# Batch 0's P V from the transposed p in place, on 32-row tiles, in an attention and gated-MLP kernel on one Trainium2 core

## The chip, the core and the metric

The kernel runs on one core of a Trainium2 chip. The core has five engines that run side by side, each with its own queue of instructions, executed in order: TensorE (PE in the profile; its weight loads are listed apart as PEld), VectorE (DVE), ScalarE (ACT), GpSimd (POOL) and SyncE (SP), which here only issues DMAs. Data lie in SBUF, on 128 partitions; matmuls write to PSUM, of which this kernel uses eight banks of 128 x 512 fp32. Engines wait for each other through semaphores. The metric is the device time of one execution in microseconds; the median of several runs is given, and one further execution is profiled.

## The reference

```python
scores = scale * np.matmul(q, k.transpose(0, 1, 3, 2))          # 8 batches, 8 heads, 576 x 64
mask_local = (rel >= 0) & (rel < 32)
mask_strided = (rel >= 0) & (pos[None, :] % 32 == pos[:, None] % 32)
masks = [mask_local if h < 4 else mask_strided for h in range(8)]
attn = softmax(where(masks, scores, -1e9))
x = (attn @ v).transpose(0, 2, 1, 3).reshape(8, 576, 512)
h = np.maximum(x @ w_in, 0.0)                                    # 512 -> 1024
u, v = h[..., :512], h[..., 512:]
v_n = (v - mean(v)) / sqrt(var(v) + 1e-6)
v_s = einsum('ts,bsd->btd', w_spatial, v_n) + b_spatial          # 576 x 576
return (u * v_s) @ w_out                                         # 512 -> 512
```

Four heads attend to a window of 32 positions back, four to the positions that are equal modulo 32. Then comes an MLP whose second half is normalised, mixed over positions and multiplied with the first.

## The kernel before

The kernel works through 8 batches. Attention is done for two heads at a time: pair `t` is batch `t // 4`, and of the four pairs of a batch the first two are local and the last two strided. So batch 0 is t = 0, 1 (local) and t = 2, 3 (strided).

A **local pair** (`local_attention`, L445) cuts the 576 queries into 18 blocks of 32. Each block needs 64 keys: its own 32 and the 32 before. The scores of the blocks are put side by side and on top of each other: five slots of columns, and within a slot up to four blocks in the four quarters of 32 partitions (`local_blocks` says which block lies where). After the softmax, p is a tile of 128 x (10 x 64). VectorE's transpose works on squares of 32 x 32 (L541) and writes the result to `pc`: each quarter then holds, transposed, the p of the blocks that lie in it. Before, this was not multiplied where it lay. Twelve copies (L548 to L562, helper `rnd`, lines L368 on ACT and L370 on DVE or POOL) moved quarters to other partitions and built `ptl`, in which 96 queries share one stationary 128 rows of v: three blocks and their four key blocks, with zeros where they don't meet. Then 12 matmuls of 128 rows, 64 columns of v and 96 queries (L570) wrote x, transposed, to two banks of PSUM, half of the queries each.

A **strided pair** (`strided_attention`, L585) has 32 residues with 18 positions each. After the transpose (L657), four copies (L661) built `pts`, block-diagonal in the same way, and 16 matmuls of 128 rows and 72 queries (L673) wrote two banks.

**Two rounded parts.** x is needed as a sum of two rounded parts, so `evac_x` (L401) makes of each bank a rounded copy (L390 or L392) and a subtraction on DVE (L378) that gives the remainder. The same splitting into two parts is done to the weights as they arrive (`weight`, L724: L746 on ACT, L754 on POOL, L762 on DVE, then `rnd` and L378): w_in arrives in eight blocks (u and v, four each), w_out in four, w_spatial in four and a tail. Each product of the MLP is then three matmuls. Every fp32 matmul of the program that isn't of this rounded type shows as two in the trace.

The **MLP** of a batch: L878 makes the v half, 128 positions a time (the last 64 positions in a tail); L920 the u half; L1001, with L1013 and L1014 for the tail, the mixing over positions, for which all of v must have been normalised and w_spatial split; L1043 multiplies with w_out. Batches overlap: attention of later batches is put between the products of earlier ones.

**What sets the order.** Nothing is ordered by hand. `Program.order` (L169) simulates the five engines with fixed costs. Each operation has a key, and an engine that is free in the simulation takes the ready operation with the lowest key. The instructions are then issued in that order; on the chip each engine's queue runs in it. The table `KEYS` (L40) gives the keys: `"a"` for the first eight pairs, `"u"`, `"v"`, `"o"` for the blocks of w_in and w_out, `"s"` and `"t"` for w_spatial, `"cst"` for the mask constants, `"fill"` for the clearing of tiles; a DMA of a pair or a weight has a key some 20 to 34 below it. `"lead"` shifts the keys of later pairs against the MLP's. Where the simulation sees PE idle for long in the first 110 us, filler matmuls on zeros are issued (L1178). The tables `tiled` and `FETCHED` hold small matmuls back where too many would follow one another.

**Buffers.** `r_po` (L357) has two banks for P V; a new user waits until both readers of the old one are done. `r_pc` has one place for the transposed p, `r_v` two for v, `r_q` two for q. `w_out_sb` (L325) is a tile of its own. t = 2 has its v in a borrowed place (`v_third`).

Of the kernel before, what the change touches and what calls it, by code (L numbers as in the profile page):

```python
# [10 lines left out]
F32R = mybir.dt.float32r  # L11
# [7 lines left out]
B, H, S, D = 8, 8, 576, 64  # L19
DM = H * D  # L20
DFF = 1024
HF = DFF // 2
P = 128
STRIDE = 32
# [5 lines left out]
LS = 5  # L30
# [8 lines left out]
NT = 4  # L39
KEYS = {  # L40
    "a": (-1153.0, -1248.4, -1132.6, -528.4, 173.8, 237.2, 196.5, 305.5,),
    "v": (-479.4, -798.9, -798.5, -237.5,),
    "u": (165.3, -36.7, -381.8, -468.5,),
    "s": (2276.1, 559.3, 2950.2, 2726.0,),
    "t": (1026.5,),
    "o": (800.1, 780.6, 949.7, 806.1,),
    "cst": (-1235.7,),
    "lead": (-1.2,),
    "fill": (261.3, 1164.3, -1850.5, -198.5, 42.5, 203.7,),
    "dp": (742, -13288,),  # L50
    "dpt": (254.9,),
    "near": (331.04,),
# [3 lines left out]
OTHER_BANK = (1, 2, 3)  # L56
FETCHED, FETCH_COST = 200.0, 32.0
# [252 lines left out]
def attention_moe(ctx, tc, qT, kT, vl, vs, cst, eye, w_in, w_out, wsp, wtail, out):  # L310
# [14 lines left out]
    w_out_sb = sb.tile([P, 2, NT, DM], F32R, name="w_out_sb")  # L325
# [27 lines left out]
    at_raw, at_minus = r_o.new(), r_o.new()  # L353
    minus = lambda: at_minus()[:, :P].bitcast(F32R)
# [41 lines left out]
    def load(key, dst, src, writes, nbytes, reads=()):  # L396
        add(key, [(DMA, nbytes / DMA_RATE)], lambda eng: eng.dma_start(dst(), src), reads, writes)
# [30 lines left out]
    def mask_scores(due, s_ps, parts):  # L428


        def f(eng):
            at = 0
            for i, k, n in parts:
                eng.matmul(
                    s_ps()[:, at : at + n * k].rearrange("p (n k) -> p n k", k=k), minus(),
                    masks(i, k)[:, None, :].to_broadcast([P, n, k]), start=at == 0, stop=False,
                )
                at += n * k

        add(  # L440
            due - 14.5, [(PE, 80 + pe_cost(P, sum(k * n for _, k, n in parts)))], f,
            [(at_minus,), (at_minus, "masks")], [(s_ps,)], spare=(s_ps, s_ps),
        )

    def local_attention(t, due, q, kl, v, vin, kin):  # L445
# [82 lines left out]
        if t in APART:  # L528
# [8 lines left out]
        pc = r_pc.new()  # L537
# [6 lines left out]
            pin, [(pc,)],  # L544
        )
        ptok = []
        ptl_c = ptl.rearrange("p (c j) q -> p c j q", j=2)
        for i, n, slot, c0, z in LOCAL_MOVES:  # L548
            for k in range(2):
                src = slice(STRIDE * z, STRIDE * (z + 1))  # L550
                dst = slice(STRIDE * (i + k), STRIDE * (i + k + 1))
                rnd(
                    due - 5, 2 * n * STRIDE,
                    lambda i=i, n=n, c0=c0, dst=dst: ptl_c[
                        dst, c0 : c0 + n, :, STRIDE * i : STRIDE * (i + 1)
                    ],
                    lambda k=k, n=n, slot=slot, src=src: turned()[
                        src, slot : slot + n, :, STRIDE * k : STRIDE * (k + 1)
                    ],
                    [(pc,), ("ptl0",)], [("ptl", i, k, c0)], blocks=True,  # L560
                )
                ptok.append(("ptl", i, k, c0))  # L562
# [22 lines left out]
    def strided_attention(t, due, q, k, v, vin, kin):  # L585
# [30 lines left out]
        if not masked:  # L616
# [36 lines left out]
        pc = r_pc.new()  # L653
# [3 lines left out]
            lambda eng: eng.transpose(turned(), pp[:]), [ptok], [(pc,)],  # L657
        )
        for i in range(4):
            r = slice(STRIDE * i, STRIDE * i + STRIDE)  # L660
            rnd(  # L661
                due - 5, nu * RA, lambda r=r, i=i: pts[r, :, i],
                lambda r=r: turned()[r, :, :RA], [(pc,), ("pts0",)], [("pts", i)], blocks=True,
            )
# [30 lines left out]
    def attention(t, due):  # L695
# [3 lines left out]
        if t == 2:  # L699
            place = v_third  # L700
            v = lambda: f32(place()).rearrange("p a b c -> p (a b c)").rearrange("p (u d) -> p u d", d=D)
        else:
            v = place = r_v.new()
        load(due - 34, q, qT[b, hp], [(q,)], P * SP * 4)
        if local:
            k = r_k.new()
            load(due - 33, k, kT[b, hp], [(k,)], P * (STRIDE + S) * 4)
            load(due - 20, lambda: v()[:, : 2 * LB, :], vl[b, hp], [(place,)], P * 768 * 4)
            kin = [(k,)]
        else:  # L710
# [5 lines left out]
            load(due - 20, v, vs[b, hp - 2], [(place,)], P * 1024 * 4)  # L716
            kin = [("k", t % 2, j) for j in range(2)]
        xs[t] = r_x.new()
        (local_attention if local else strided_attention)(t, due, q, k, v, [(place,)], kin)

    def x_tok(t):
        return [(xs[t], i, c0) for i in range(2) for c0 in ((0, 3) if t % NHP < 2 else (0, 1))]
# [49 lines left out]
    def weights():  # L772
        jobs = []
        for i in range(NT):
            rows = slice(i * P, (i + 1) * P)
            for c, name in enumerate("uv"):
# [6 lines left out]
                KEYS["o"][i], w_out[rows, :], DM, lambda j, i=i: w_out_sb[:, j, i], ("w_out", i),  # L783
# [4 lines left out]
        for job in jobs:  # L788

            def put(job=job):  # L790
                what = "w_out" if job[4][0] == "w_out" else "w_in"
# [9 lines left out]
            yield job[0], put  # L801
# [181 lines left out]
    def moe_2(b, key):  # L983
# [50 lines left out]
        def project(hf, k0):  # L1034
            c0 = b * S + hf * HS
            g = gs.pop(hf)
            for e in range(NT):
                o_ps = r_pm.new()
                for f in range(NT):

                    def fn(eng, e=e, f=f, o_ps=o_ps):
                        for i, (w, a) in enumerate(PROD):
                            eng.matmul(  # L1043
                                o_ps()[:, :HS],
                                w_out_sb[:, w, f, e * P : (e + 1) * P],
# [7 lines left out]
                        [(g[0], f), (g[1], f), ("w_out", f, 0), ("w_out", f, 1)], [(o_ps,)],  # L1053
# [133 lines left out]
def _layout(q, k, v, w_in, w_spatial, b_spatial, w_out):  # L1187
# [21 lines left out]

    cst = np.zeros((P, 3, 2 * STRIDE), np.float32)  # L1210
# [7 lines left out]
    def words(w):  # L1218
# [12 lines left out]
        "vl": vl,  # L1231
        "vs": vs,
# [26 lines left out]
```

## Time and profile before

| | |
|---|---|
| median of 3 runs | 529.55 us (527.65 to 531.61) |
| the profiled execution | 528.65 us |
| its span, first to last instruction | 526.9 us |
| mean granted TensorE clock | 0.997 |
| ACT, POOL busy | 244.5, 85.7 us |
| share of the chain that ended last | L1043 20%, L1001 19%, L920 17%, L878 17% |

The chain of work that ended last is PE's for 88% of the span. The profile gives each engine's busy time in any stretch of the span, its instructions in order of time (with the idle time ahead of one and what ended it, in brackets), and groups of instructions by line and shape. In the timeline a row is: start, length, engine, line, operation, output<-inputs, shape, count. A row that merges several instructions has the time from the first start to the last end. "issue" in brackets means that the engine waited for nothing that the profile shows.

### The profile page before, as it was taken

To read this page: it belongs to the slowest core of one execution; us is meant where nothing else is said; L and a number is where in the kernel's file an instruction comes from. 1 tells how busy PE (TensorE), PEld (TensorE's weight loads), DVE (VectorE), ACT (ScalarE), POOL (GpSimd) and SP (SyncE) were. 2 spreads that over 40 slices of the span, in tenths; PEclk is the share of its full clock that TensorE was granted. 3 is DMA by queue.
4 is the path that set the end of the run, shared out by engine and by line. 5 is a ranking of instruction groups with operands and counts; after the bars stand their busy time and mean duration, and the time that the engine had idled before them with its cause. 6 is when DMAs were issued, how large, how long until landed. Compare 5 with 4: busy or idle time off the path is not lost.

```text
span 526.9 us, 14624 instructions
## 1 busy us (share of the span) xinstructions
PE 514.0 (98%) x6002; PEld 471.0 (89%) x6002; DVE 317.1 (60%) x1004; ACT 244.5 (46%) x753; POOL 85.7 (16%) x170
## 2 busy tenths in 40 slices
PE   8899899899999999999999999999999999999997
PEld 4569699789899898998999899998999899998997
DVE  3999997594862867716256677954268252426132
ACT  6769665556553664724433473522234242213111
POOL 1643421121120213201010032111002020001000
PEclk9999899999999999999999999999999999999999
DMA  7978633622252223410223324310022200110011
GB/s 260 323 271 259 220 110 101 207 92 90 70 171 81 89 84 121 164 46 0 79 79 123 111 79 163 117 46 24 0 73 70 85 1 1 46 46 1 1 46 45
DMA packets 26242, 52.65 MB, mean 100 GB/s; under 512 B 3136, under 2 KB 11584, under 8 KB 26176
## 3 DMA queue, kind: packets, MB, share of 16 engines
q1 hardware_dynamic: 26176, 51.72, 29.6%
q8 instruction: 47, 0.77, 0.6%
q14 instruction: 19, 0.16, 0.1%
HBM read 42.27 MB, written 9.44 MB: 98 GB/s over the span
## 4 chain that ended last, share of the span: by engine, by line
PE 88%; DVE 7%; ACT 2%; issue 1%; DMA 1%; POOL 1%; DVEq 0%; ACTq 0%; POOLq 0%
PE m L1043 20%; PE m L1001 19%; PE m L920 17%; PE m L878 17%; PE po L673 3%; PE po L570 3%; PE s L460 2%; PE m L1013 2%; PE s L603 2%; PE m L1014 2%; PE m L1178 1%; DVE w_in_sb L378 1%; DMA q<-qT 1%; DVE vn L378 1%; ACT pl L517 1%
## 5 line engine op out<-in xcount | busy, mean ns | idle before, releaser
L1001 PE MATMUL m<-wsp_sb,vn 128*128 128x288 f32 x768 | 112.7, 298 | 2.0 <-DVE wsp_sb L378 1.5
L1001 PEld LDWEIGHTS m<-wsp_sb,vn 128*128 128x128 f32 x768 | 106.5, 191 | 3.2 <-DVE wsp_sb L378 2.0
L1043 PE MATMUL m<-g,w_out_sb 128*128 128x288 f32 x768 | 106.6, 297 | 0.0
L920 PE MATMUL m<-x,w_in_sb 128*128 128x288 f32 x768 | 106.2, 297 | 0.0
L920 PEld LDWEIGHTS m<-x,w_in_sb 128*128 128x128 f32 x768 | 103.3, 188 | 1.6
L1043 PEld LDWEIGHTS m<-g,w_out_sb 128*128 128x128 f32 x768 | 103.5, 188 | 0.6
L878 PE MATMUL m<-w_in_sb,x 128*128 128x512 f32 (+1 forms) x408 | 100.0, 398 | 2.1 <-issue 1.4
L878 PEld LDWEIGHTS m<-w_in_sb,x 128*128 128x128 f32 (+1 forms) x408 | 74.2, 185 | 22.9 <-issue 2.4
L390 ACT COPY o<-m 128x288 f32<-128x288 f32 x60 | 23.8, 399 | 90.3 <-PE m L1043 73.0
L854 POOL TENSOR_TENSOR bn<-bn,sel 128x1 f32<-128x1 f32 (+1 forms) x37 | 20.7, 560 | 188.4 <-DVE bn L849 185.0
L378 DVE TENSOR_TENSOR x<-po,x 128x288 fp32r<-128x288 f32 x64 | 27.5, 447 | 38.5 <-ACT x L390 38.1
L1023 DVE TENSOR_TENSOR u<-m,u 128x288 f32<-128x288 f32 x64 | 28.1, 452 | 37.2 <-PE m L1014 36.8
L370 POOL TENSOR_SCALAR ptl<-pc 32x320 f32<-32x320 f32 (+3 forms) x71 | 29.0, 408 | 128.4 <-PE po L570 69.2
L517 ACT ACTIVATE pl<-pl,ml 128x64 f32<-128x64 f32 (+1 forms) x140 | 47.0, 338 | 3.6 <-DVE ml L497 3.6
L841 DVE BATCH_NORM_STATS2 bn<-vv 128x6 f32<-128x512 f32 (+1 forms) x37 | 25.5, 688 | 36.0 <-ACT vv L836 35.8
L934 ACT ACTIVATE u<-m 128x288 f32<-128x288 f32 x64 | 26.2, 409 | 40.6 <-PE m L920 40.3
L836 ACT ACTIVATE vv<-m 128x512 f32<-128x512 f32 (+1 forms) x37 | 22.0, 595 | 45.0 <-PE m L878 43.8
L390 ACT CAST x<-po 128x288 fp32r<-128x288 f32 x57 | 21.8, 399 | 22.4 <-PE po L570 12.6
L378 DVE TENSOR_TENSOR g<-u,g 128x288 fp32r<-128x288 f32 x64 | 28.1, 453 | 6.0 <-ACT g L368 5.1
L861 DVE TENSOR_SCALAR vv<-vv,bn 128x512 f32<-128x512 f32 (+1 forms) x37 | 20.4, 552 | 16.0 <-POOL bn L854 15.9
L368 ACT COPY ptl<-pc 32x320 f32<-32x320 f32 (+3 forms) x72 | 25.7, 357 | 3.7 <-DVE pc L541 2.5
L368 ACT CAST g<-u 128x288 fp32r<-128x288 f32 x39 | 16.2, 433 | 23.7 <-DVE u L1023 22.8
(127 smaller groups left out, 579.2 us busy)
## 6 DMA issues: line engine op xcount, KB each, us to landing
q<-qT SPq DMA_DIRECT2D x32, 295.0 KB, 4.2
outT<-o SPq DMA_DIRECT2D x64, 144.0 KB, 1.8
v_raw<-vs SPq DMA_DIRECT2D x15, 512.0 KB, 3.9
v_raw<-vl SPq DMA_DIRECT2D x16, 384.0 KB, 3.6
k<-kT SPq DMA_DIRECT2D x16, 304.0 KB, 4.6
kbd<-kT SPq DMA_DIRECT2D x32, 144.0 KB, 4.1
vn<-w_in SPq DMA_DIRECT2D x4, 512.0 KB, 7.5
x<-wsp SPq DMA_DIRECT2D x4, 288.0 KB, 7.5
```

The source lines that it names most:

```text
L368: eng.copy(dst(), src())
L370: eng.tensor_scalar(dst(), src(), 1.0, 0.0, op0=ALU.mult, op1=ALU.add)
L378: eng.tensor_tensor(dst(), src(), f32(hi()), op=ALU.subtract)
L390: eng.copy(dst(), src())
L517: eng.activation(p_sb()[:m, u, :], src, AF.Exp, bias=st()[:m, u : u + 1], scale=SCALE if masked else -1.0, **total,)
L841: lambda eng: eng.bn_stats(bn()[:m, 0:6], v()[:m]), [(v,)], [(bn,)],
L878: eng.matmul(v_ps()[:m, :], x_at(kt)[:, a, :], w_in_sb[:, w, kt, HF:], start=(n == 0 and i == 0), stop=(n == NT - 1 and i == 2),)
L920: eng.matmul(u_ps()[:, :HS], w_in_sb[:, w, kt, f * P : (f + 1) * P], xs[NHP * b + kt]()[:, a, r], start=(n == 0 and i == 0), stop=(n == NT ...
L934: lambda eng, u=u, f=f, u_ps=u_ps: eng.activation(u()[:, f * HS : (f + 1) * HS], u_ps()[:, :HS], AF.Relu),
L1001: eng.matmul(s_ps()[:, :HS], vn()[:, a, kt, fs], wsp_sb[:, w, kt, r], start=(kt == 0 and i == 0), stop=False,)
L1023: lambda eng, ug=ug, s_ps=s_ps: eng.tensor_tensor(ug(), s_ps()[:, :HS], ug(), op=ALU.mult),
L1043: eng.matmul(o_ps()[:, :HS], w_out_sb[:, w, f, e * P : (e + 1) * P], g[a]()[:, f, :], start=(f == 0 and i == 0), stop=(f == NT - 1 and i = ...
```

## The change

For the pairs in `DIRECT`, which are the four of batch 0, the copies to `ptl` and `pts` go, and P V reads the transposed p where it lies. Each of the four quarters of partitions is a group of matmuls of its own, with 32 rows, and writes a bank of its own out of `r_po`; the quarter's bank is then evicted by its own pair of copy and subtraction. A local block takes two matmuls a head (its two halves of the keys, added up in PSUM) of 32 columns; a strided residue takes one of 18. All other batches stay as they were.

v of the two local pairs is laid out to suit (`vq`, built on the host): 32-row pieces in the quarter where the p they meet lies, 20 x 64 numbers a partition instead of 12 x 64. This v, and two places for the transposed p of batch 0, lie in the room of w_out, which is now a ring of one: `early_in` is its first user and `w_out_at` its second. So w_out's parts are written only after batch 0's P V has read the room. r_v and r_pc have fewer users. All keys have new values.

```diff
 KEYS = {
-    "a": (-1153.0, -1248.4, -1132.6, -528.4, 173.8, 237.2, 196.5, 305.5,),
-    "v": (-479.4, -798.9, -798.5, -237.5,),
-    "u": (165.3, -36.7, -381.8, -468.5,),
-    "s": (2276.1, 559.3, 2950.2, 2726.0,),
-    "t": (1026.5,),
-    "o": (800.1, 780.6, 949.7, 806.1,),
-    "cst": (-1235.7,),
-    "lead": (-1.2,),
-    "fill": (261.3, 1164.3, -1850.5, -198.5, 42.5, 203.7,),
+    "a": (-1491.5, -1499.5, -1376.8, -1072.3, 275.6, 126.4, 366.6, 331.6,),
+    "v": (-1350.3, -1394.1, -928.4, -858.3,),
+    "u": (-85.1, -24.1, 10.9, -892.8,),
+    "s": (2014.4, 679.4, 3723.6, 3023.6,),
+    "t": (1957.7,),
+    "o": (1155.8, 2305.5, 1386.0, 979.5,),
+    "cst": (-2368.6,),
+    "lead": (8.39,),
+    "fill": (1008.5, 2319.1, -2366.4, 1990.2, -234.6, 1525.4,),
...
+DIRECT = (0, 1, 2, 3)
...
+def quadrant_blocks(z):
+    slots = ((slot, local_blocks(slot)) for slot in range(LS))
+    return [(slot, found[z]) for slot, found in slots if z < len(found)]
...
+    r_wo = Ring(sb, "w_out_sb", [P, 2, NT, DM], F32R, 1)
+    early_in, w_out_at = r_wo.new(), r_wo.new()
+    def room(first, n):
+        return f32(early_in()).rearrange("p a b c -> p (a b c)")[:, first : first + n]
...
+    def turned_room(t):
+        if t not in DIRECT:
+            pc = r_pc.new()
+            return pc, (pc,)
+        return (lambda: room(2 * NVQ + NPC * (t % 2), NPC)), (early_in, "pc", t % 2)
...
+        if t in DIRECT:
+            for z in range(4):
+                blocks, o_ps = quadrant_blocks(z), r_po.new()
+                w = STRIDE * len(blocks)
...
+                rows = slice(STRIDE * z, STRIDE * (z + 1))
+                def f_v(eng, blocks=blocks, o_ps=o_ps, at=at, rows=rows):
+                    for slot, r in blocks:
+                        for k in range(2):
+                            for j in range(2):
+                                eng.matmul(
+                                    o_ps()[D * j : D * j + D, at(slot, r) : at(slot, r) + STRIDE],
+                                    v()[rows, (2 * slot + k) * 2 + j, :],
+                                    turned()[rows, slot, j, STRIDE * k : STRIDE * (k + 1)],
+                                    start=k == 0, stop=k == 1,
+                                )
...
+                evac_x(due, x_t, o_ps, w, z, src, dst)
+            return
...
+        if t in DIRECT:
+            for i in range(4):
+                o_ps = r_po.new()
+                rows = slice(STRIDE * i, STRIDE * (i + 1))
+                def f_v(eng, o_ps=o_ps, rows=rows):
+                    for c in range(SB):
+                        for j in range(2):
+                            eng.matmul(
+                                o_ps()[D * j : D * j + D, RA * c : RA * (c + 1)],
+                                v()[rows, 2 * c + j, :], turned()[rows, 2 * c + j, :RA],
+                                start=True, stop=True,
+                            )
...
-            yield job[0], put
+            yield max(job[0], max(KEYS["a"][:NHP])) if job[4][0] != "w_in" else job[0], put
```

In both attention functions `pc, ptok_c = turned_room(t)` takes the place of `pc = r_pc.new()`, and `ptok_c` that of `(pc,)`.

More of the change, by code (lines that the diff above doesn't have):

```diff
@@ L309, in attention_moe @@
 @with_exitstack
-def attention_moe(ctx, tc, qT, kT, vl, vs, cst, eye, w_in, w_out, wsp, wtail, out):
+def attention_moe(ctx, tc, qT, kT, vl, vq, vs, cst, eye, w_in, w_out, wsp, wtail, out):
     nc = tc.nc
@@ L559, in local_attention @@
                     ],
-                    [(pc,), ("ptl0",)], [("ptl", i, k, c0)], blocks=True,
+                    [ptok_c, ("ptl0",)], [("ptl", i, k, c0)], blocks=True,
                 )
@@ L790, in put @@
             def put(job=job):
-                what = "w_out" if job[4][0] == "w_out" else "w_in"
+                what = "w_in" if job[4][0] == "w_in" else "w_out"
                 n = count[what]
```

74 lines of the change are left out of this document (57 added, 17 removed).

## The prediction

> **What bounds the kernel now.** I read the page first, then busy time by stretch, then the timelines of PE, DVE and SP, and the chain that ended last.
>
> ```profile
> span 526.9 us, 14624 instructions
> PE 514.0 (98%) x6002; PEld 471.0 (89%) x6002; DVE 317.1 (60%) x1004; ACT 244.5 (46%) x753; POOL 85.7 (16%) x170
> ...
> 0.00:5.00 5.00, 4.06 (x10) 1.78 (x11) 1.49 (x7) 4.27 (x5) 2.29 (x7) 1.00 0.63 204
> 5.00:10.00 5.00, 5.00 (x129) 3.24 (x130) 0.95 (x4) 0.88 (x4) 0.00 (x0) 1.00 0.82 293
> ...
> 22.00:59.00 37.00, 36.07 (x448) 29.12 (x450) 35.77 (x90) 28.80 (x77) 19.89 (x29) 1.00 0.82 280
> 59.00:69.00 10.00, 8.04 (x84) 7.29 (x79) 9.63 (x38) 7.40 (x25) 1.60 (x3) 0.83 0.34 102
> ```
>
> Columns of a stretch: from:to, length, busy time of PE, PEld, DVE, ACT, POOL, granted clock, DMA share, GB/s. PE is 98% busy over the span, but up to 22 us much of that is filler. From 22 to 59 us DVE is busy 35.77 of 37.00 us, as full as PE, and from 59 to 69 us it is fuller (9.63 against 8.04) while the clock drops to 0.83. So the start is DVE's. Where does PE wait for it?
>
> ```profile
> 18.73 1.28 PE L570 MATMUL po<-ptl,v_raw 128*64 128x96 f32 x24 [1.04 <-ACT ptl L368]
> ...
> 21.95 2.10 PE L878 MATMUL m<-w_in_sb,x 128*128 128x512 f32 x6
> ...
> 44.86 9.86 PE L920 MATMUL m<-x,w_in_sb 128*128 128x288 f32 x72
> ...
> 59.47 0.40 PE L1001 MATMUL m<-wsp_sb,vn 128*128 128x288 f32 x1
> 60.65 1.33 PE L1001 MATMUL m<-wsp_sb,vn 128*128 128x288 f32 x8 [0.78 <-DVE wsp_sb L378]
> 62.39 0.40 PE L1001 MATMUL m<-wsp_sb,vn 128*128 128x288 f32 x1 [0.41 <-ACT wsp_sb L368]
> 63.55 5.44 PE L1001 MATMUL m<-wsp_sb,vn 128*128 128x288 f32 x29 [0.76 <-DVE wsp_sb L378]
> ```
>
> Dense work (batch 0's first product, L878) begins at 21.95. It meets DVE at 59.47: the spatial product waits three times for split w_spatial, and its 39 matmuls end at 63.55 + 5.44 = 68.99. At L920's pitch (9.86/72 = 0.137 us) they need 5.3 us, so they might as well have begun at 63.6. I call 63.6 the effective start, and whatever moves it moves the end, because afterwards PE runs nearly unbroken. The exception I count is this hole:
>
> ```profile
> 101.11 0.50 PE L878 MATMUL m<-w_in_sb,x 128*128 128x512 f32 x1
> 103.04 1.20 PE L878 MATMUL m<-w_in_sb,x 128*128 128x512 f32 x4 [1.42 <-issue]
> ...
> q8 instruction: 47, 0.77, 0.6%
> ```
>
> **What PE needs up to there.** Rows for the price of one matmul:
>
> ```profile
> 57.42 1.21 PE L570 MATMUL po<-ptl,v_raw 128*64 128x96 f32 x24
> 58.56 0.97 PE L460 MATMUL s<-k,q 64*32 64x64 f32 x72
> ...
> 71.19 1.22 PE L673 MATMUL po<-pts,v_raw 128*64 128x72 f32 x32
> 72.34 0.77 PE L603 MATMUL s<-kbd,q 128*32 128x36 f32 x64
> ...
> L570 PE MATMUL po<-ptl,v_raw 128*64 128x96 f32 x384 | 19.7, 251 | 2.3 <-issue 1.3 <-ACT ptl L368 1.0
> L673 PE MATMUL po<-pts,v_raw 128*64 128x72 f32 x480 | 18.3, 229 | 0.2 <-issue 0.2
> L673 PEld LDWEIGHTS po<-pts,v_raw 128*64 128x64 f32 x480 | 16.1, 137 | 3.2 <-issue 2.4 <-POOL pts L370 0.6 <-DVE u L1023 0.2
> L460 PE MATMUL s<-k,q 64*32 64x64 f32 x1080 | 14.5, 224 | 0.0
> L603 PE MATMUL s<-kbd,q 128*32 128x36 f32 x896 | 10.3, 199 | 0.0
> ...
> 233.48 11.21 PE m L878 x48
> ...
> 483.04 12.80 PE m L920 x96
> ```
>
> Between 21.95 and 59.47 (37.5 us) lie 48 L878 (11.2), 96 L920 (12.8), the tail's 12 half-width L878 (12 x 0.2335 = 2.8), four P V (t0, t2, t3 and batch 1's first; 1.15 each, start to next start, 71.19 to 72.34) and three sets of scores (0.9, 0.9, 0.75): 34.0 us. The slack is 3.5 us.
>
> **The P V matmuls.** Pitch in a run is (length - one duration)/(count - 1), with the mean durations of the groups by shape: L570 (96 columns, 64-column load) (1.21 - 0.251)/23 = 42 ns, L673 (72, 64) 32, L460 (64, 32) 10.5, L603 (36, 32) 9.1. Every fp32 matmul of the program is two in the trace, so a local pair goes from 24 to 144 instructions (18 blocks x 2 heads x 2 key halves x 2; 32 columns each), a strided pair from 32 to 128 (18 columns). Unseen: a 64-column load on 32 rows with so few columns. From below: the line through L570 and L673 gives 2.9 + 0.40 N, so 16 ns at 32 columns and 10 at 18. From above, for a load that costs twice what a 32-column one does: 21 and 18 ns. I take 18 and 14, about the middles, as neither end is nearer. Four groups instead of one start the pipe three times more, 0.16 us each (1.15 - 31 x 0.032), 0.5 us a pair. So a local pair is 144 x 0.018 + 0.5 + 0.16 = 3.25, a strided 128 x 0.014 + 0.66 = 2.45. The extra behind 21.95 is 2.1 (t0) + 1.3 + 1.3 = 4.7 us; t1's 2.1 lies ahead of it, where PE runs fillers. The ends: 3.4 and 6.1.
>
> [...]
>
> **Instruction fetch.** 432 more matmuls with as many loads are 864 instructions; the instruction queue moved 0.77 MB in 47 packets for 2 x 6002 on PE, about 255 a packet, so 3.4 packets more. The hole at 101.6 (1.42 us) follows four runs of small matmuls. Between 0 and 3.4 x 1.42 = 4.8 us; I take one hole, 1.4. PE could then reach the spatial product at 59.47 - 3.5 - 2.0 (first x earlier, below) + 6.1 = 60.1.
>
> **The copies.** Work of batch 0 on ptl and pts:
>
> ```profile
> 10.00:41.00 31.00, 2.49 (x48) 2.11 (x48) 1.40 (x3) 3.87 (x11) 4.65 (x10) 1.00 0.87 298
> ...
> 10.00:41.00 31.00, 2.66 (x64) 2.28 (x64) 0.00 (x0) 2.17 (x5) 2.29 (x3) 1.00 0.87 298
> ...
> 24.59 0.71 DVE L657 STREAM_TRANSPOSE pc<-pp 128x512 f32<-128x512 f32 x1 [0.47 <-POOL ptl L370]
> ```
>
> All 32 go: 1.40 us of DVE, 6.0 of ACT, 6.9 of POOL. Only DVE's is on the bounding engine; ACT and POOL have room in 22 to 59 (28.80 and 19.89 of 37). DVE's wait of 0.47 for the single pc goes too, since batch 0 now has two places.
>
> **The evictions.** Each pair's two pairs of copy and subtraction become four, of 160, 160, 128 and 128 columns (local) or 4 x 144.
>
> ```profile
> L378 DVE TENSOR_TENSOR x<-po,x 128x288 fp32r<-128x288 f32 x64 | 27.5, 447 | 38.5 <-ACT x L390 38.1
> ...
> L378 DVE TENSOR_TENSOR vn<-vv,vn 128x512 fp32r<-128x512 f32 x32 | 22.0, 691 | 1.7 <-ACT vn L368 1.4
> ```
>
> Slope (691 - 447)/224 = 1.09 ns a column, fixed part 133 ns. Two more subtractions a pair cost 2 x 133 ns, 1.1 us over four pairs; back to back they overlap a little, I take 0.8 (0.5 to 1.1). ACT's added copies fit in what it was freed of. Copies, wait and evictions together: -1.40 - 0.47 + 0.8 = -1.1 us of DVE, between -2.0 (with flexible roundings leaving DVE) and +0.3 (eight new handovers of 0.05 to 0.1 us and the wait back). The four groups share two banks, so the third waits until the first is copied and subtracted: about 1 us, with scores or L878 of an earlier pair queued between. What stands behind it on PE if DVE is late is every later matmul; that risk is in the range.
>
> **The new order.** SP's queue now begins with the mask constants, then q and k of t1 and t0, then both v, then the first w_in block (-1394.1 - 25 = -1419.1) ahead of t2's q (-1376.8 - 34 = -1410.8).
>
> ```profile
> 6.38 0.31 ACT L1102 ACTIVATE o<-cst_sb 128x128 fp32r<-128x128 f32 x1 [1.12 <-DMA cst_sb<-cst]
> ...
> 9.05 0.89 DVE L480 TENSOR_REDUCE ml<-m 128x5 f32<-128x320 f32 x2 [6.37 <-PE m L460]
> ...
> 9.08 0.33 SPq L397 DMA_DIRECT2D q<-qT  x1
> 9.94 1.78 SPq L397 DMA_DIRECT2D vn<-w_in  x2
> ...
> 15.80 0.83 DVE L541 STREAM_TRANSPOSE pc<-pl 128x640 f32<-128x640 f32 x1
> 16.79 0.65 POOL L754 TENSOR_SCALAR vn<-vn 128x512 int32<-128x512 uint8 x1 [13.90 <-DMA vn<-w_in]
> ...
> v_raw<-vl SPq DMA_DIRECT2D x16, 384.0 KB, 3.6
> ```
>
> The mask, late by 1.12 us, comes sooner, and with it the first scores: -1.0 us (0 to -1.6). The first w_in, which sits behind t2's q on SP and reaches POOL at 16.79, can land before 13 us, when DVE has holes between reductions: -1.0 (0 to -1.2). Both v grow from 384 to 640 KB, 0.5 MB, 1.7 us at 298 GB/s; the DMA's idle 2.75 us of the first ten (shares 0.63 and 0.82) hides that, and without this cover the second -1.0 is gone. t2's q comes up to 1.7 us later; DVE has t1 and t0 to do meanwhile, so nothing. x of t1 then comes 2.0 us sooner: 1.0 from the masks and 1.0 from PE starting at the transpose's end (16.63) instead of 2.1 us later (18.73), less the wait for a bank. w_out is split after batch 0's P V instead of any time before 61 us: nothing, only the projection behind the spatial product reads it. Clearing ptl and pts may come later: nothing, batch 1 is their first user. From the third batch on, attention is due 9.6 us sooner (lead 8.39 for -1.2); PE runs unbroken there, so I take nothing, and 2 us either way in the range.
>
> **The sum.** DVE: -1.1 - 1.0 - 1.0 = -3.1, so the effective start is 63.6 - 3.1 = 60.5; PE's own 60.1 is just under it. The profiled execution took 528.65 us (span 526.9 + 1.75 around it): 525.5. The median shown, 529.55, is 0.9 higher: 526.4 us.
>
> **Rivals.** (F) DVE gains all it can (-2.0 - 1.6 - 1.2 = -4.8) and the hole at 101.6 closes (-1.4): -6.2, 523.3. For it: PE without a fetch hole arrives at 58.7, early enough. Against: DMA is 0.87 busy from 10 to 41 us, and earlier loads crowd one another. (N) DVE's relief is spent again on evictions, bank waits and DMA: 529.5. For it: ACT and POOL, not DVE, carried 29 of the 32 copies. (S) Slower: the pitch of a matmul with a 64-column load does not fall with its columns. PE decides once the extra passes 63.6 - 54.0 = 9.6 us, that is 400 p + 2.0 - 3.45 = 9.6 (144 + 2 x 128 instructions, three pairs' starts, less the three old runs), p = 28 ns. At L673's 32 ns it is 11.3 us, +1.7; at L570's 42 it is 15.3, +5.7 and 535.2. For it: no row shows a 64-column load under 32 ns. Against: those two rows follow their columns (42/32 = 1.31 against 96/72 = 1.33), which a load limit wouldn't. [...]
>
> **How the numbers follow.** Forecast 0.4, F 0.25, N 0.2, S 0.15. Runs of the kernel before spread from 527.65 to 531.61, so about 1% (5.3 us) can be told from no change. Faster by over 1% (under 524.3): F and a little of the forecast, 0.28. Slower (over 534.9): most of S, 0.12. The rest, 0.60. The range reaches from F's deeper end less 2 us of order, 521, to S at 32 ns with 2 us of bank waits, 533.
>
> **What would show it.** Right: the P V runs at 13 to 20 ns; no ptl or pts work before 45 us; first L878 near 20 us; the spatial product's 39 matmuls ended near 66 us, with waits below 1 us. Wrong: PE idle ahead of a third group, waiting for DVE on po; P V pitch over 28 ns; issue holes within 16 to 40 us; w_in landing no sooner than 16 us.

## The result, and the profile after

The changed kernel takes 552.08 us (median of 4 runs, 549.47 to 555.27) against 528.94 us before (4 runs, 527.65 to 531.61): a ratio of 1.043, with a 95% interval of 1.036 to 1.050. The forecast was 526.4 us with a range to 533. The profiled execution took 552.96 us, its span is 24.3 us longer than the span before.

The page of the changed kernel, first its span and busy times, then the granted clock over 40 slices of 13.8 us, then the instruction queue:

```profile
span 551.2 us, 15425 instructions
...
PE 538.2 (98%) x6422; PEld 492.7 (89%) x6422; DVE 311.8 (57%) x993; ACT 240.1 (44%) x743; POOL 87.3 (16%) x175
...
PEclk9755999999999999999999999999999999999999
...
q8 instruction: 50, 0.82, 0.6%
```

PE is 98% busy, as before, and 24.2 us longer (538.2 against 514.0). A busy PE that takes longer has either more work or slower work. The row of the clock says which to look at first: 7, 5, 5 in the second to fourth slice, 9 elsewhere. The same in stretches (columns as in the prediction):

```profile
15.00:20.00 5.00, 3.65 (x163) 3.45 (x163) 3.96 (x8) 1.17 (x3) 0.69 (x1) 0.97 1.03 409
...
20.00:57.00 37.00, 35.70 (x512) 29.49 (x512) 16.22 (x36) 10.80 (x26) 3.88 (x6) 0.50 0.30 114
...
57.00:58.00 1.00, 1.00 (x31) 0.97 (x29) 0.00 (x0) 0.00 (x0) 0.00 (x0) 0.86 0.00 0
```

From 20 to 57 us PE is busy for 35.70 of 37 us at a granted clock of 0.50. DVE, which was to be the bound there, is busy for 16.22 us. Before, the same 37 us and the place behind them read:

```profile
20.00:57.00 37.00, 35.65 (x449) 28.59 (x448) 35.77 (x91) 30.40 (x81) 19.76 (x30) 1.00 0.85 291
60.00:63.00 3.00, 1.73 (x9) 1.28 (x9) 3.00 (x6) 2.63 (x6) 0.00 (x0) 1.00 0.91 270
63.00:66.00 3.00, 2.45 (x10) 2.46 (x11) 3.00 (x11) 0.96 (x3) 1.32 (x3) 0.52 0.16 56
66.00:67.00 1.00, 1.00 (x8) 1.00 (x7) 0.97 (x13) 1.00 (x4) 0.27 (x1) 0.74 0.00 0
```

Same busy PE, same length, twice the clock. Before had a short fall too, behind PE's waits at 60 to 63.5 us. Its length follows from the column: (0.48 x 3 + 0.26 x 1) / 0.5 = 3.4 us at half speed, then the clock is back. After, it stays away for 37 + (0.03 x 5 + 0.14) / 0.5 = 37.6 us, eleven times 3.4. What PE did there, from its timeline in the changed kernel (L579 is the in-place local P V, L722 the in-place strided one, L965, L1007 and L1088 are the former L878, L920 and L1001, L658 the former L603):

```profile
14.93 2.32 PE L579 MATMUL po<-w_out_sb 32*64 32x32 f32 x80 [0.76 <-DVE ml L427]
17.18 0.77 PE L658 MATMUL m<-kbd,q 128*32 128x36 f32 x64
17.88 0.76 PE L579 MATMUL po<-w_out_sb 32*64 32x32 f32 x19
21.30 5.74 PE L579 MATMUL po<-w_out_sb 32*64 32x32 f32 x125 [2.65 <-issue]
...
28.55 3.23 PE L579 MATMUL po<-w_out_sb 32*64 32x32 f32 x64
31.71 1.19 PE L658 MATMUL m<-kbd,q 128*32 128x36 f32 x64
32.83 1.65 PE L965 MATMUL m<-w_in_sb,x 128*128 128x512 f32 x3
34.41 3.21 PE L722 MATMUL po<-w_out_sb,xt 32*64 32x18 f32 x64
...
44.36 2.93 PE L965 MATMUL m<-w_in_sb,x 128*128 128x512 f32 x6
...
57.95 5.16 PE L965 MATMUL m<-w_in_sb,x 128*128 128x512 f32 x21
62.95 3.36 PE L1007 MATMUL m<-x,w_in_sb 128*128 128x288 f32 x24
...
82.89 3.40 PE L1088 MATMUL m<-wsp_sb,vn 128*128 128x288 f32 x22
```

Three things are to be seen. The first 80 of the local matmuls, at full clock, take 17.18 - 14.93 = 2.25 us, 28 ns each; later 64 take 31.71 - 28.55 = 3.16 us, 49 ns each. In between stands one idle time of 2.65 us, ended by "issue", behind 163 small matmuls in a row, and the clock falls within it (0.87 in the microsecond from 19, 0.50 in the next). And from 20 us on no row of the stretch has a wait for DVE or ACT: the engine that was the bound isn't on the path any more.

### The profile page after: what moved, and what is told of

Same layout as the page of the kernel before. It is cut to its first block, busy times and chain, and to the rows that moved or that the text cites. A ratio compares the mean times of both kernels' runs of the same rounds, so it can differ in the third digit from the quotient of the medians.

```text
span 551.2 us, 15425 instructions
## 1 busy us (share of the span) xinstructions
PE 538.2 (98%) x6422; PEld 492.7 (89%) x6422; DVE 311.8 (57%) x993; ACT 240.1 (44%) x743; POOL 87.3 (16%) x175
## 4 chain that ended last, share of the span: by engine, by line
PE 86%; DVE 9%; ACT 2%; issue 2%; POOL 1%; ACTq 0%; POOLq 0%
PE m L965 20%; PE m L1130 18%; PE m L1007 17%; PE m L1088 14%; PE po L752 3%; PE po L722 2%; PE po L625 2%; PE po L579 2%; PE s L481 2%; PE s L658 1%; PE m L1100 1%; PE m L1101 1%; PE m L1265 1%; DVE ptl L384 1%; DVE u L1110 1%
## 5 line engine op out<-in xcount | busy, mean ns | idle before, releaser
L1088 PE MATMUL m<-wsp_sb,vn 128*128 128x288 f32 x768 | 112.8, 296 | 0.2 <-DVE bn L936 0.2
L1088 PEld LDWEIGHTS m<-wsp_sb,vn 128*128 128x128 f32 x768 | 105.4, 189 | 1.7 <-DVE bn L936 0.4
L1007 PE MATMUL m<-x,w_in_sb 128*128 128x288 f32 x768 | 105.8, 297 | 0.0
L965 PE MATMUL m<-w_in_sb,x 128*128 128x512 f32 (+1 forms) x408 | 105.4, 415 | 0.0
L1007 PEld LDWEIGHTS m<-x,w_in_sb 128*128 128x128 f32 x768 | 103.5, 188 | 1.4
L965 PEld LDWEIGHTS m<-w_in_sb,x 128*128 128x128 f32 (+1 forms) x408 | 77.4, 194 | 19.0
L392 DVE TENSOR_TENSOR x<-po,x 128x288 fp32r<-128x288 f32 (+3 forms) x72 | 30.0, 432 | 47.0 <-ACT x L404 46.3
L404 ACT CAST x<-po 128x288 fp32r<-128x288 f32 (+3 forms) x67 | 25.6, 385 | 55.4 <-PE po L722 18.3
L384 POOL TENSOR_SCALAR ptl<-pc 32x320 f32<-32x320 f32 (+3 forms) x66 | 27.0, 409 | 92.0 <-PE po L625 74.2
L384 POOL TENSOR_SCALAR pts<-pc 32x288 f32<-32x288 f32 x29 | 13.9, 479 | 95.6 <-PE po L752 59.6
L538 ACT ACTIVATION_READ_ACCUMULATOR pl<-pl,ml 128x1 f32 (+1 forms) x140 | 26.4, 188 | 0.0
```

Source lines behind the costliest of these rows:

```text
L384: eng.tensor_scalar(dst(), src(), 1.0, 0.0, op0=ALU.mult, op1=ALU.add)
L392: eng.tensor_tensor(dst(), src(), f32(hi()), op=ALU.subtract)
L404: eng.copy(dst(), src())
L538: eng.activation(p_sb()[:m, u, :], src, AF.Exp, bias=st()[:m, u : u + 1], scale=SCALE if masked else -1.0, **total,)
L965: eng.matmul(v_ps()[:m, :], x_at(kt)[:, a, :], w_in_sb[:, w, kt, HF:], start=(n == 0 and i == 0), stop=(n == NT - 1 and i == 2),)
L1007: eng.matmul(u_ps()[:, :HS], w_in_sb[:, w, kt, f * P : (f + 1) * P], xs[NHP * b + kt]()[:, a, r], start=(n == 0 and i == 0), stop=(n == NT ...
```

## The experiments

The main theory, C: matmuls on 32 rows count for little in whatever sets the clock, so a long run of them lowers it, and short runs of dense matmuls between them don't raise it. Its rivals: O, the new order makes the loss; the hole at 18.6 us alone does it; the pitch of 64-column loads (rival S of the prediction); the start of the kernel, where the DMAs are full. H, of the later runs, splits C into a fall and a holding. The "window" of the expectations is the length of 3.4 us that before's fall shows; that the clock is set window by window is part of the theory and is not shown by itself. Spans are compared with the order alone, which has the same keys.

### The order without the change, and the change without the order

```diff
-DIRECT = (0, 1, 2, 3)
+DIRECT = ()
```

> The changed kernel with its new keys, but P V of batch 0 by the old way (copies to ptl and pts, 128-row matmuls). Theory C (the 32-row matmuls keep TensorE at half clock): no long stretch at 0.5, 526 to 531 us. Theory O (the new order of loads starves the start, whatever P V does): still a hole of over 2 us near 19 us, the clock at 0.5 for tens of us, and 540 us or more. Theory P (the price of P V alone, 27 ns a matmul in place of 18): as C, 526 to 531 us.

529.76 us (10 runs) against 529.27, ratio 1.003 (0.9995 to 1.006). Its timeline of PE where batch 0's second product begins:

```profile
39.26 3.34 PE L1007 MATMUL m<-x,w_in_sb 128*128 128x288 f32 x24
```

and its stretches:

```profile
20.00:57.00 37.00, 35.05 (x452) 29.47 (x451) 34.11 (x87) 27.84 (x71) 18.98 (x26) 0.95 0.78 277
25.00:30.00 5.00, 3.96 (x38) 3.34 (x39) 4.93 (x14) 3.68 (x9) 2.73 (x4) 0.69 1.00 353
```

The order alone makes no difference that can be measured; O falls. It also has a fall of the clock at 27 us, behind a wait of 1.92 us, but only of one 3.4 us length. L1007 begins at 39.26 us against 62.95: 23.7 us, and the spans differ by 23.3 (551.2 - 527.9). So the whole loss is made before L1007.

The other half, `KEYS` as before with `DIRECT` kept:

> The changed kernel with the keys of before: P V in place, old priorities. Theory C: the clock again goes to 0.5 for 20 us or more between 16 and 60 us and the time is 540 to 555 us. Theory O: no hole and no long slow stretch, 530 to 535 us (only the dearer P V, about +4 us). Theory P: 531 to 535 us at full clock.

560.17 us (4 runs), 1.059 (1.055 to 1.063): the loss is there in the old order as well. The clock is 0.53 from 20 to 50 us and L1007 begins at 62.91 us. PE then loses more at 130 to 150 us (busy for 14.96 of 20 us, mostly waiting for DVE and a DMA), which the new keys don't have.

### The same matmuls on 128 rows

```diff
-    v()[rows, (2 * slot + k) * 2 + j, :],
-    turned()[rows, slot, j, STRIDE * k : STRIDE * (k + 1)],
+    v()[:, (2 * slot + k) * 2 + j, :],
+    turned()[:, slot, j, STRIDE * k : STRIDE * (k + 1)],
...
-    v()[rows, 2 * c + j, :], turned()[rows, 2 * c + j, :RA],
+    v()[:, 2 * c + j, :], turned()[:, 2 * c + j, :RA],
```

> The changed kernel with each P V matmul of batch 0 reading all 128 rows of the same two tiles instead of its 32 (so x of batch 0 holds sums over other quarters too); count, columns, banks and order stay. Theory C: the hole near 19 us and the drop stay, but the clock is back to 1 within two windows of about 3.4 us, and the time is 530 to 538 us. A theory in which the gap alone matters, or the pitch alone: no change, 549 to 555 us.

543.12 us (2 runs), 1.027 (1.021 to 1.033). Same order, same count, a hole like the other, and a pitch that is longer, not shorter (64 of L579 take 3.56 us at half clock, against 3.16). The run behind the hole, from the timeline of PE:

```profile
20.90 6.83 PE L579 MATMUL po<-w_out_sb 128*64 128x32 f32 x125 [2.40 <-issue]
```

and two stretches:

```profile
33.00:34.00 1.00, 1.00 (x65) 0.92 (x57) 1.00 (x2) 0.18 (x1) 0.00 (x0) 0.50 0.00 0
...
35.00:40.00 5.00, 5.00 (x105) 3.96 (x104) 2.58 (x8) 2.37 (x7) 0.00 (x0) 1.00 0.38 123
```

The clock falls here too, at 21.1 us, just behind the hole, so behind matmuls on 128 rows, too, a hole of 2.40 us was enough. But it is back at 34.7 us, 22.6 us sooner than on 32 rows, and stays at 1.00 through the same alternation of L722 and L965. That is what C says. It took four lengths of 3.4 us to come back, more than expected, and so the time misses what was expected of it. Through the first two of them PE ran 125 small matmuls on 128 rows without a break, and the clock stayed at 0.50: the number of rows isn't all that counts.

### The suspect by itself: trains of small matmuls

In the kernel before, ahead of a v tile of batch 3 and of batch 5, where PE otherwise runs dense, 256 matmuls (512 in the trace) on constants, with no wait and nobody who reads them; `rows` is 0 to 31 in batch 3 and 0 to 127 in batch 5:

```diff
+        for i in range(256):
+            nc.tensor.matmul(
+                buf()[D * (i % 2) : D * (i % 2) + D, :32],
+                cst_sb[rows, 0], cst_sb[rows, 1, :32], start=True, stop=True,
+            )
```

> The kernel before with two trains of 256 fp32 matmuls each (512 in the trace), 64-column loads and 32 moving columns, put ahead of the second v tile of batch 3 (operands on 32 rows) and of batch 5 (the same on 128 rows), in dense stretches. Theory C: within 3.4 to 7 us of its start the 32-row train falls from clock 1 to 0.5 and its pitch from 27 to about 50 ns, the 128-row train stays at 1. Theory that only a gap lowers the clock: both stay at 1 and 27 ns, about 14 us each.

The trains in the timeline of PE:

```profile
239.10 25.60 PE L1192 MATMUL m<-cst_sb 32*64 32x32 f32 x512
...
389.83 15.12 PE L1192 MATMUL m<-cst_sb 128*64 128x32 f32 x512
```

and the stretches from the start of the first, and most of the second:

```profile
238.00:240.00 2.00, 2.00 (x36) 1.50 (x36) 0.16 (x1) 0.60 (x1) 0.00 (x0) 1.00 0.08 24
240.00:242.00 2.00, 2.00 (x67) 2.00 (x64) 1.20 (x4) 0.00 (x0) 0.55 (x1) 0.86 0.00 0
242.00:244.00 2.00, 2.00 (x42) 2.00 (x42) 0.22 (x1) 0.00 (x0) 0.00 (x0) 0.50 0.00 0
...
385.00:400.00 15.00, 15.00 (x376) 14.17 (x376) 2.00 (x5) 1.40 (x3) 0.55 (x1) 1.00 0.10 33
```

PE is busy for all of both trains. On 32 rows the clock is at 0.50 from 2.3 us after the start (0.86 over 240 to 242 us is half speed from 241.4 on) until 4 us after the end, and the train takes 25.60 us; on 128 rows it stays at 1.00 and the same count takes 15.12. So being busy alone didn't hold the clock at 1.00; the two trains differ in the rows at work, and in their batch. Each train ran once. The kernel took 574.55 us (1 run), the trains' own time included.

### One half of the change alone

`DIRECT = (0, 1)`, the local pairs, and `DIRECT = (2, 3)`, the strided ones:

> The changed kernel with only the two local pairs in place, the strided ones by copies. Theory C: half clock from the hole near 19 us until the local P V are over and one window of dense matmuls has passed, some 12 to 15 us; 534 to 542 us. If the hole is what matters: as the whole change, 548 us or more.

> The changed kernel with only the two strided pairs in place. Theory C: even without a hole of over 2 us the clock goes to 0.5 while quarters of 32 rows alternate with short runs of L965, 15 us or more, 534 to 545 us. If a hole is needed: full clock, 528 to 532 us.

541.14 us (2 runs), 1.020 (1.016 to 1.023), and 552.77 us (2 runs), 1.042 (1.036 to 1.047). The local half, by stretch:

```profile
20.00:35.00 15.00, 13.57 (x267) 11.87 (x269) 6.49 (x17) 4.87 (x13) 2.42 (x4) 0.50 0.69 249
```

and the strided half:

```profile
26.00:40.00 14.00, 14.00 (x173) 11.06 (x169) 8.90 (x20) 6.00 (x13) 3.28 (x5) 0.54 0.57 217
```

Either half does it. The local half falls at its hole (2.77 us) and comes back at 36.8 us, just behind the start of 18 L965 in a row (36.66 us); L1007 begins at 48.02 us, 8.8 later than in the order alone. The strided half falls at 27 us, behind a wait of 1.37 us and where the order alone falls too, but stays low to 40.7 us, four lengths instead of one; L1007 begins at 50.09 us, 10.8 later. So by L1007 the strided half costs only 2 us more than the local one. That its total is 11.6 us higher, and beyond the 545 us expected, comes mostly from elsewhere: between 80 and 100 us PE is busy for 11.2 of 20 us, with one wait of 5.5 us for DVE, which no other run has there. Why, stays open.

### Away from the start

Strided pairs of batches 3, 4 and 5 in place instead (`DIRECT = (14, 15, 18, 19, 22, 23)`), far from the crowded start; p then lies in its usual place:

```diff
-        if t not in DIRECT:
+        if t not in DIRECT or t > 3:
             pc = r_pc.new()
```

> The changed kernel with six strided pairs of batches 3 to 5 (t = 14, 15, 18, 19, 22, 23) in place and none of batch 0: the same quarters of 32 rows, but in the dense part, where each stands among long runs of MLP matmuls. Theory C: a quarter's 0.9 us in a window of about 3.4 us is too little to lower the clock, which stays at 1 there; dearer by about 0.6 x 4 us a pair at 27 ns at most, 530 to 545 us. If any 32-row run lowers it: half clock around each of the six, 545 us or more.

564.94 us (1 run). One of the pairs in the timeline of PE:

```profile
189.03 1.84 PE L722 MATMUL po<-pc,v_raw 32*64 32x18 f32 x64
190.80 0.97 PE L481 MATMUL s<-k,q 64*32 64x64 f32 x72
191.70 0.67 PE L1007 MATMUL m<-x,w_in_sb 128*128 128x288 f32 x3
192.30 3.15 PE L722 MATMUL po<-pc,v_raw 32*64 32x18 f32 x64
```

and the stretches around it:

```profile
189.00:192.00 3.00, 3.00 (x139) 2.85 (x139) 1.71 (x6) 1.25 (x3) 0.55 (x1) 1.00 0.03 5
192.00:195.00 3.00, 3.00 (x63) 2.83 (x62) 0.87 (x2) 0.40 (x1) 0.00 (x0) 0.57 0.66 201
```

The start isn't needed, and no idle time is either: PE is busy for all of these six microseconds, and the clock falls at 192.4 us, as the second run of L722 begins. The expectation that it would hold there was wrong: two quarters, a set of scores and 0.67 us of dense work are already too little. Idle times ended by "issue" come here as well (1.71 us at 159.7, 2.71 at 231.1 us), each behind some 200 small matmuls in a row, and with the DMAs 0.70 and 0.83 busy in the six microseconds around them. The trains, with 512 in a row (at 29 ns on 128 rows, with a DMA share of 0.10), had none: it is not the number alone.

### What brings the clock back

Fillers on zeros (128 rows, 256 columns, the kernel's own L1265) in two places of the changed kernel: eight (16 in the trace) once, ahead of batch 0's first L965, and two ahead of each quarter of the local pairs.

The lines of the two runs, with comments added:

```diff
+    if n == 0 and extra:                       # first run: once, extra = 8
+        prog.more[len(prog.ops) - 1] = (v_ps, extra)
...
+    prog.more[len(prog.ops) - 1] = (o_ps, 2)   # second run: each local quarter
...
+    if n in self.more:                         # in emit, ahead of operation n
+        warm(*self.more[n])
```

> The changed kernel with 8 more filler matmuls (16 in the trace, 256 columns each) ahead of the first L965, 6.8 us at half clock, so that the clock comes back before the quarters alternate with L965. Theory H (the alternation only holds the clock where it is: it cannot raise it from 0.5, nor lower it from 1): the clock stays at 1 behind the fillers and the time is 538 to 546 us. Theory C as first put (the alternation itself lowers it): 0.5 again within two windows, 555 to 560 us.

> The changed kernel with two filler matmuls (four in the trace, 0.85 us at full clock) ahead of each quarter of the two local pairs, which gives the fetch of instructions time and the array work. Theory H with the hole as its trigger: no hole over 1.5 us near 19 us, at most one window of half clock before 45 us, 530 to 540 us. Theory C as first put: half clock again while the strided quarters run, 545 us or more.

546.71 us (3 runs), 1.029 (1.022 to 1.036), and 546.07 us (3 runs), 1.032 (1.024 to 1.039). Stretches of the first, and two rows of its timeline of PE (L582 is the in-place local P V):

```profile
15.00:20.00 5.00, 3.73 (x153) 3.48 (x149) 3.44 (x7) 1.47 (x4) 1.74 (x2) 0.73 1.02 350
30.00:35.00 5.00, 5.00 (x76) 3.17 (x74) 0.29 (x1) 0.59 (x2) 0.64 (x1) 0.90 0.14 52
35.00:45.00 10.00, 10.00 (x244) 8.04 (x240) 7.53 (x18) 4.31 (x11) 0.00 (x0) 1.00 0.21 66
...
17.46 1.27 PE L582 MATMUL po<-w_out_sb 32*64 32x32 f32 x19
20.88 5.75 PE L582 MATMUL po<-w_out_sb 32*64 32x32 f32 x125 [2.14 <-issue]
```

and of the second:

```profile
20.00:39.00 19.00, 19.00 (x416) 13.89 (x412) 9.10 (x25) 5.87 (x16) 3.89 (x6) 1.00 0.64 231
39.00:44.00 5.00, 5.00 (x63) 3.91 (x60) 2.50 (x5) 1.28 (x4) 0.00 (x0) 0.66 0.01 2
44.00:51.00 7.00, 7.00 (x107) 5.46 (x107) 4.07 (x8) 3.90 (x10) 0.00 (x0) 0.76 0.01 2
```

The first shows what lowers the clock at the start. The hole lasts from 18.73 to 20.88 us, but 0.73 over 15 to 20 us is half speed from 17.3 us on, 1.4 us ahead of the hole, and the 19 matmuls at 17.46 us already take 1.27 us instead of the 0.76 in the changed kernel. Under the old keys, too, the clock falls behind 99 of these matmuls with 0.46 us of idle time. So the rival that the hole alone does it falls: the run on 32 rows was enough here. In the changed kernel itself the clock falls 1.1 us into the hole, and which of the two did it there can't be told.

5.9 us of fillers, from 26.55 us on, raise the clock at about 31 us, and then the very alternation that stayed at 0.50 in the changed kernel runs at 1.00 (it falls once more, from about 48 us on). With fillers inside the local runs there is no hole and no fall until 40 us, and in the strided alternation the clock then falls with PE busy, twice, for 0.34 x 5 / 0.5 = 3.4 us each. So the loss has two parts: something that lowers the clock (the run on 32 rows, or a hole), and an alternation that keeps whatever clock it finds, most of the time. With the fillers' own time included both runs are 5 to 6 us faster than the changed kernel, and slower than before. The second misses the 530 to 540 us expected, and H in its strict form, in which the alternation cannot lower the clock, doesn't hold.

This gives the price of half a clock. From the 64 local matmuls at 28.55 us to the six L965 at 44.36 us the changed kernel needs 15.81 us; the first filler run needs 9.02 for the same sequence at 1.00 (33.24 to 42.26). The stretch is 1.75 times as long, not 2.

### Several row groups at once

If rows at work count, quarters that take turns matmul by matmul should help, and be faster too. First all four (four banks at a time, `banks = [(r_pm if z > 1 else r_po).new() for z in range(4)]`), then two and two; and the latter with two fillers ahead of a pair of quarters (`prog.more[...] = (banks[0], 2)`), and with the keys of before. The loop of two and two, shortened:

```diff
+    for slot in slots:
+        for k in range(2):
+            for j in range(2):
+                for y, o in zip((z, z + 1), banks):   # two quarters in turn
+                    eng.matmul(o()[D * j : D * j + D, at : at + STRIDE], ...
```

> The changed kernel with the four quarters of a pair taken in turn, matmul by matmul, each into its own of four banks (two of po, two of m), so that neighbours stand on different rows; the count of matmuls, the keys and the evictions stay, one P V operation a pair. Theory C, refined (the clock follows how much of the array's rows works): four quarters at once count as much as 128 rows, pitch under 15 ns, at most one window of half clock after a hole, 525 to 535 us. If the clock only counts instructions or columns: half clock as before, 545 us or more.

> The changed kernel with the quarters of a pair taken two at a time, matmul by matmul in turn, into the same two banks of po (64 rows at work instead of 32); keys, count and evictions stay. Theory C with the load rate (two row groups load and run side by side): pitch 13 to 16 ns at full clock, the quarters' time halves, and half clock lasts at most 15 us; 532 to 542 us. If the pitch is per instruction whatever the rows: 27 ns, and 545 to 555 us.

> The quarters two at a time (as paired) and two filler matmuls ahead of each of the four operations of the local pairs, as in fill2: both remedies together. Theory H: no hole over 1.5 us, full clock but for at most one window before 45 us, P V at 14 to 16 ns; 530 to 538 us, the first in-place version within 1.5% of the kernel before. If two row groups at once still let the clock fall by themselves: 540 us or more.

> The same with the keys of before. Theory C: better than the 560.2 us of the changed matmuls under these keys by 10 us or more; whether the new or the old order suits it better is open, 530 to 550 us.

| | median (runs) | ratio (95%) | ns a matmul, full clock | half clock in the first 57 us |
|---|---|---|---|---|
| as changed | 552.08 (4) | 1.043 (1.036 to 1.050) | 28 | 20 to 57 |
| four in turn | 557.58 (4) | 1.050 (1.046 to 1.053) | 11 | 20 to 33, 47 to 50 |
| two in turn | 546.93 (4) | 1.033 (1.025 to 1.040) | 16 | 21 to 38, 45 to 55 |
| two, fillers | 543.12 (5) | 1.025 (1.020 to 1.031) | 17 | 22 to 32, 42 to 56 |
| two, keys of before | 549.73 (2) | 1.039 (1.032 to 1.046) | not read | in parts from 15 on |

The pitch halves, as the first rows of two in turn show (timeline of PE; 16.58 - 15.28 = 1.30 us for 80):

```profile
15.28 1.37 PE L582 MATMUL po<-w_out_sb 32*64 32x32 f32 x80 [0.76 <-DVE ml L427]
16.58 0.77 PE L662 MATMUL m<-kbd,q 128*32 128x36 f32 x64
...
22.12 1.50 PE L582 MATMUL po<-w_out_sb 32*64 32x32 f32 x47 [2.51 <-issue]
```

The hole stays, and the clock still falls at it. New waits of 0.3 to 1.0 us for evictions of the two banks come in. Four in turn came back at 33 us, but all 48 of its L965 start only at 47.29 us; I put that down to the two banks taken from m's ring, which is argued and not tested. None of these beats the kernel before, and three of them miss what was expected: 525 to 535 us for four in turn, 532 to 542 for two, and 530 to 538 for two with fillers, by 5 us. All of them have idle times of 1 to 3 us where the clock falls or is low, so they don't tell whether row groups in turn would hold it.

A last test of rows by themselves, in the kernel before again: a train over two row groups in turn, and a train of 32-row runs of 1 us with 1 us of fillers between.

```diff
+    z = (i // 2) % 2 if kind == "two" else 0
+    rows = slice(32 * z, 32 * z + 32)
...
+    if kind == "mix" and i % 16 == 15:
+        warm(more, 2)
```

> As the earlier trains, in dense stretches of the kernel before: at batch 3, 512 instructions that alternate between two groups of 32 rows and two banks; at batch 5, 288 of 32 rows in runs of 32 (about 0.9 us), each followed by two filler matmuls (128 rows, 32 columns loaded, 256 moving, four instructions, about 0.9 us). Theory C: the mix falls to half clock within about two windows although nothing is idle, as batch 0 of the change does; the two groups run at 13 to 16 ns, and if the clock follows rows at work at that pace they keep it at 1 (if it needs more than 64 rows, 0.5). If only a gap starts the drop: the mix stays at 1.

The mix in the timeline of PE:

```profile
371.74 1.12 PE L1196 MATMUL m<-cst_sb 32*64 32x32 f32 x32
372.79 1.05 PE L1186 MATMUL po<-zeros 128*32 128x256 f32 x4
```

and a stretch from its last third:

```profile
384.00:386.00 2.00, 2.00 (x38) 1.33 (x38) 0.00 (x0) 0.00 (x0) 0.00 (x0) 1.00 0.00 0
```

Half the time on dense work held the clock at 1.00 for 18 us; the expectation that it would fall was wrong. The changed kernel's alternation (at half clock some 1.6 us of L965 to 1.9 or 3.2 us of L722) did not regain it from 0.50. The two-group train ran at 15 ns but had three issue holes of together 1.5 us and fell to 0.50 at about 235.2 us; whether 64 rows at once would hold the clock without holes is left open. The kernel took 563.83 us (1 run).

## Why the prediction was wrong

**The step that failed** is "PE could then reach the spatial product at ... 60.1". Every duration behind that number was a full-clock one. In the changed kernel the first L1088 runs at 82.89 us, 22.8 later. Where these come from, worked out and not measured separately:

- The clock, in no term of the sum: 21.30 to 57.95 us is 36.65 us; divided by 1.75 it is 20.9, so 15.7 us.
- The pitch: 28 ns against 18 and 14. In the prediction's own sum, 400 x 0.028 + 2.0 - 3.45 = 9.75 us instead of 4.7, so 5.0 us.
- The hole ended by "issue": 2.65 us against 1.4, so 1.3 us.

Together 22.0; 0.8 us is left, of which 0.55 are waits of a later batch for ptl (81.0 to 81.7 us). Against the effective start of before that is 82.9 - 63.6 = 19.3 us, and the span grew by 24.3. The other 5 us are not fully assigned. Idle times ended by "issue" behind 82.9 us sum to 3.3 us against 2.7. Counted from the first L1007 (L920 before, at 40.84 us), 22.1 of the 24.3 us lie ahead of it; the order alone begins it 1.6 us sooner than before and yet ends 1.0 us later, so 2.6 us behind it are lost with the new order and the old P V as well.

As a check from another kernel: the second filler run begins L1007 at 55.53 us. Less seven pairs of fillers ahead of quarters (0.98 us each from start to start, 6.9) and two falls (6.8 us of half clock, of which 0.75/1.75 is loss: 2.9), this is 45.7 us, 6.5 after the order alone. The changed kernel's 23.7 less clock (15.7) and hole (2.65) leaves 5.4. The two agree to about a microsecond.

**Rival S** had the right mechanism for the pitch. The pitch doesn't follow the columns: 64 matmuls of 32 columns take 1.79 us (33.24 to 35.03) and 64 of 18 columns 1.77 (36.62 to 38.39) in the first filler run, 28 ns both. Its break-even was 28 ns, so by itself it would have left the time about where it was. That sum leaves out the hole of 1.4 us which the forecast takes; with it, break-even is 24 ns, and 28 ns costs 1.5 us. Either way it is not what made the kernel 23 us slower. Both ends that the 18 and 14 lie between were too low: the line through L570 and L673 takes a column price from matmuls of 72 and 96 columns, which fewer columns don't follow, and twice a 32-column load gave 21 and 18 ns. L603's 9.1 ns, the lower of the two prices that were doubled, doesn't carry over: its loads have 32 columns, and four matmuls in turn write four different quarters of the result. The 64-column loads take 28 ns on one row group, 16 with two groups in turn and 11 with four.

**What was right, and worth nothing.** The first scores began 1.0 us sooner (7.06 instead of 8.05 us), and the first w_in reached POOL at 13.17 instead of 16.79 us. All 32 copies are gone. The evictions cost what the slope said for 160 and 128 columns and some more for 144; the timeline of DVE in the changed kernel:

```profile
16.66 0.32 DVE L392 TENSOR_TENSOR x<-po,x 128x160 fp32r<-128x160 f32 x1
...
22.58 0.29 DVE L392 TENSOR_TENSOR x<-po,x 128x128 fp32r<-128x128 f32 x1 [3.31 <-ACT x L404]
...
36.79 0.40 DVE L392 TENSOR_TENSOR x<-po,x 128x144 fp32r<-128x144 f32 x1 [2.62 <-ACT x L404]
```

In the stretch DVE waits for PE and ACT by whole microseconds, and L1088 waits 0.2 us for it in all. What DVE's relief is worth can't be read from a kernel in which PE comes 20 us too late. With the order alone DVE is busy for 34.11 of 37 us and still near the bound, and there the 2.0 us forecast for earlier masks and w_in don't show at the end.

**Of the signs named ahead**, "no ptl or pts work before 45 us" and the sooner w_in held; pitch over 28 ns and issue holes within 16 to 40 us came; the first L965 at 26.97 us was far from 20. The clock was not among the signs and no rival named it, although the row of 59 to 69 us in the prediction showed 0.83 behind idle time of PE: it was mentioned there and given no term.

## What to carry to other kernels

Before matmuls are cut to fewer rows, price them at half the clock as well: here a TensorE busy on a quarter of its rows fell to 0.50 within 2.3 us, idle times of 1.92 and 2.40 us were followed by the same fall, and the dense work behind it ran for some 4.1 us (the train) and 4.5 us (the fillers) before the clock was back. Look at the granted clock of each stretch before any wait: the changed kernel's PE is 98% busy, as before, with the clock at 0.50 for 37.6 us. And a pitch taken from matmuls with 32-column loads that take turns says nothing of 64-column loads that stay in one row group (9.1 against 28 ns here).

## What the hardware showed unexpectedly

- The clock fell with PE fully busy on 32 rows: 0.50 within 2.3 us of the start of a pure train; 1.00 throughout for the same train on 128 rows, and for 1 us on 32 rows against 1 us of fillers.
- The stretches at 0.50 lasted multiples of 3.4 us (3.4 before, 13.6 on 128 rows, 37.6 in the changed kernel), and the same alternation was seen in either state: three L965 in turn with 32 or 64 matmuls on 32 rows stayed at 0.50 from 28 to 57 us in one kernel and at 1.00 from 33 to 48 us in another.
- Half the granted clock made the same sequence 1.75 times as long (15.81 against 9.02 us).
- Small matmuls with 64-column loads in one row group took 28 ns whether 18 or 32 columns ran through (29 to 31 on all 128 rows); two groups in turn 15 to 17 ns, four 11.
- After some 150 to 210 small matmuls in a row PE stopped for 1.4 to 2.8 us with nothing to wait for, where the DMAs were 0.70 to 1.03 busy. With a DMA share of 0.13 or less a train of 512 at 29 ns had no such hole, one at 15 ns had three, and four in turn, at 11 ns, had one of 1.43 us. With fillers ahead of each quarter there was none (PE busy for 19.00 of 19 us from 20 us on). That it is the fetch of instructions is an inference: the profile only says "issue", and the instruction queue's packets rose from 47 to 50.
